# Row loads of the last third in 128 equal runs, and four weight columns copied two steps later, in a Fourier-transform and gated-product kernel

## The chip, the cores and the metric

The kernel runs on one core of one Trainium2 chip. The metric is device time in microseconds (us) of one execution. Where several executions are quoted, the number is their median. The profile of a kernel is one execution of it, and its span is some 1.7 to 2.8 us shorter than the device time of that execution.

## The reference, cut to what matters

```python
# x: (8, 3008, 256) f32; w_in: (256, 2048) f32; w_out: (2048, 256) f32
X = np.fft.fft(np.fft.fft(x, axis=1), axis=2).real.astype(np.float32)
t = X.reshape(8 * 3008, 256)
h = t @ w_in
g = h * np.cos(h)
return (g @ w_out).astype(np.float32)
```

## The kernel before

Both Fourier transforms are done as matmuls in f32. The transform over the 256 channels is folded into w_in ahead of time: TensorE multiplies w_in by cosines and sines, which gives Wc and Ws ("fold_sin", "fold_cos"). The transform over the 3008 rows is a set of matmuls against constant matrices MC. VectorE first folds each row with its mirror rows, so that a quarter of the rows, 752, is left to transform. After that come 376 steps, most of them 4.75 us long. A step makes two blocks of h, the cosine, the product and the second matmul.

Row s of a quarter lies on partition p in slot m. The first 512 rows lie four to a partition. The last third (rows 512 to 767, of which those after 752 are zeroed in MC) lies in two halves of 64 partitions. The function that says so, the mask that goes with it, and the load:

```python
def _row_of(m):
    p = np.arange(128)
    return 4 * p + m if m < 4 else 512 + 4 * (p % 64) + 2 * (p // 64) + m - 4

    low = np.arange(128) < 64          # in _dft_consts: the rows with v = row % 4 < 2
# ... cut ...
    def load_x(b, gather=True):
        # ... cut: tiles; GpSimd gathers the two mirrored sides (indirect loads) ...
        for j, row in ((0, 0), (3, HALF)):
            pin(eng.dma_start(out=L[j][:, 0 : 4 * ND], in_=xrows(b, row, 4, 128, 4)))
            pin(eng.dma_start(
                    out=L[j][:, 4 * ND :],
                    in_=bass.AP(tensor=xt, offset=x.offset + (b * SEQ + row + 512) * ND,
                        ap=[[2 * ND, 2], [4 * ND, 64], [1, 2 * ND]])))
```

The outer dimension of that last pattern has size 2: two sets of 64 runs of 2 rows (2 KB). The loads are issued on SyncE's queue (SP) in this order: half of w_in, the four row loads of batch 0, the other half of w_in, two of the constant matrices, w_out, the other two.

Channel 128 has no partition left in the 128-row array. Its weights are the last row of Ws. Small DMAs issued by GpSimd (POOL) turn that row into columns, "wex". They stand inside fold_sin, so POOL meets them in program order:

```python
    def fold_sin(q, tag="H"):
        ps = fold_mms(q, 128, tag)
        act(Ws[:, q * 512 : (q + 1) * 512], ps)
        for f in range(4):
            c = q * 512 + f * 128
            pin(nc.gpsimd.dma_start(out=wex[q][:, f : f + 1], in_=Ws[127:128, c : c + 128]))
```

POOL also makes weight sums ("WT") and, in every step, four sums of G that TensorE waits for. The rows of channel 128 come by a chain of loads on SP. It loads one channel element by element, writes it to DRAM and reads it back in the layout of the rows ("xs"). The first read is cut in two because of the two halves above:

```python
        def copy(j, s0, s1, row, step):        # in load_ext: x1 <- x, 8 partitions each
            spin(out=rows[j][:, s0:s1], in_=bass.AP(tensor=xt,
                    offset=x.offset + row * ND + 128,
                    ap=[[SEQ * ND, NB], [step * ND, s1 - s0], [1, 1]]))
        # ... cut: five such copies, four of them of 768 elements for each of 8 batches ...
            for j in range(4):                  # in turn_ext
                spin(out=xe_dr[j], in_=rows[j][:, 0:768])
            for j in range(4):
                spin(out=xs[:, j, :, 0:4], in_=xe_dr[j][:, 0:512].rearrange("b (p m) -> p b m", m=4))
                pairs = xe_dr[j][:, 512:768].rearrange("b (q h m) -> h q b m", h=2, m=2)
                for h in range(2):
                    spin(out=xs[64 * h : 64 * h + 64, j, :, 4:6], in_=pairs[h])
```

This chain feeds one fold on POOL ("xs<-xs") and one transform on TensorE ("MC,xe") in step 12. Wherever I write "the channel-128 chain", I mean these loads on SP.

Of the kernel before, what the change touches and what calls it, by code (L numbers as in the profile page):

```python
# [18 lines left out]
SEQ = 3008  # L19
ND = 256  # L20
# [16 lines left out]
def _row_of(m):  # L37

    p = np.arange(128)
    return 4 * p + m if m < 4 else 512 + 4 * (p % 64) + 2 * (p // 64) + m - 4  # L40


def _dft_consts():

    low = np.arange(128) < 64
    every = low | True
    out = np.zeros((128, 4, MW), np.float64)
    for kodd in range(2):
        for ri in range(2):
            fn = np.cos if ri == 0 else np.sin  # L50
            c = 0
            for m, keep, n in (
                (0, every, NH),
                (4, low, NH),
                (2, every, NH),
                (4, ~low, NH),
                (1, every, NE),
                (3, every, NE),
                (5, every, NE),
            ):  # L60
                s = _row_of(m)
                k = 2 * np.arange(n) + kodd
                v = fn(2.0 * np.pi * ((s[:, None] * k[None, :]) % SEQ) / SEQ)
                v[s > RUN] = 0.0
                v[s == 0] *= 0.5
                v[s == RUN] *= 0.5 if ri == kodd else 0.0
                v[~keep] = 0.0
                out[:, 2 * kodd + ri, c : c + n] = v
                c += n
    return out.reshape(128, -1).astype(np.float32)  # L70
# [22 lines left out]
def _row_consts():  # L93

    neg = SEQ - _row_of(3)
    last = neg.copy()
    last[0] = SEQ - 4
    return np.stack(
        [neg, SEQ - _row_of(5), HALF - _row_of(3), HALF - _row_of(5), last], axis=1
    ).astype(np.uint32)  # L100
# [3 lines left out]
def kernel(  # L104
# [11 lines left out]
    n_tiles = (n_cols + TW - 1) // TW  # L116

    MC_dr = nc.inline_tensor(_dft_consts(), name="dft_mats")
    CC_dr = nc.inline_tensor(_chan_consts(), name="chan_mats")
    PK_dr = nc.inline_tensor(_pick_consts(), name="pick_mats")  # L120
# [14 lines left out]
    xt = x.tensor  # L135

    def xrows(b, row, step, n, rows=6):

        return bass.AP(
            tensor=xt,  # L140
            offset=x.offset + (b * SEQ + row) * ND,
            ap=[[step * ND, n], [1, rows * ND]],
        )
# [6 lines left out]
    def gather_x(b, L, j, short):  # L150

        if short:
            c, part = 2 * j - 1, slice(0, 2 * ND)
        else:
            c = 4 if j == 1 and b == NB - 1 else 2 * j - 2
            part = slice(2 * ND, 6 * ND)
        pin(
            nc.gpsimd.indirect_dma_start(
                out=L[j][:, part],
                out_offset=None,  # L160
                in_=xflat,
                in_offset=bass.IndirectOffsetOnAxis(ap=ix[:, c : c + 1], axis=0),
                element_offset=b * SEQ * ND,
            )
        )

    def spin(**kw):
        pin(nc.sync.dma_start(**kw))  # L168
# [3 lines left out]
    def load_x(b, gather=True):  # L172
        L = [
            spool.tile([128, 6 * ND], FP, tag=f"xl{j}", bufs=1, name=f"xl{j}")
            for j in range(4)
        ]
        if gather:
            for j, short in GATHERS:
                gather_x(b, L, j, short)
        eng = nc.gpsimd if b == 1 else nc.sync  # L180
        for j, row in ((0, 0), (3, HALF)):
            pin(eng.dma_start(out=L[j][:, 0 : 4 * ND], in_=xrows(b, row, 4, 128, 4)))
            pin(
                eng.dma_start(
                    out=L[j][:, 4 * ND :],
                    in_=bass.AP(
                        tensor=xt,
                        offset=x.offset + (b * SEQ + row + 512) * ND,
                        ap=[[2 * ND, 2], [4 * ND, 64], [1, 2 * ND]],
                    ),  # L190
                )
            )
        return L
# [23 lines left out]

    load_w1(0)
    L_first = load_x(0)
    load_w1(1)  # L220

    def w1_cols(h, c0, c1):
        half = c0 // 1024
        return w1[h, half][:, c0 - half * 1024 : c1 - half * 1024]
# [3 lines left out]
    for kodd in range(2):  # L228
        for ri in range(2):
            m = cpool.tile([128, MW], FP, tag=f"MC{ri}{kodd}", name=f"MC{ri}{kodd}")  # L230
# [3 lines left out]
        if kodd == 0:  # L234
            spin(
                out=w2.rearrange("p (q c) -> p q c", c=ND),
                in_=moe_w_out.rearrange("(q p) c -> p q c", p=128),
# [22 lines left out]
    xe_dr = dpool.tile([4, NB, 768], FP, tag="xe", name="xe_dr")  # L260
    r4_dr = dpool.tile([1, NB], FP, tag="r4", name="r4")

    def bank(tag):
        bufs = 3 if tag == "H" else 1
        return ppool.tile([128, 512], FP, tag=tag, bufs=bufs, name=tag)
# [3 lines left out]
    def mm(out_, lhsT, rhs, start, stop=True):  # L269
        pin(  # L270
            nc.tensor.matmul(  # L271
                out_, lhsT=lhsT, rhs=rhs, start=start, stop=stop, skip_group_check=True
            )
        )
# [7 lines left out]
    def act(o, i, func=AF.Copy, **kw):  # L282
        pin(nc.scalar.activation(out=o, in_=i, func=func, **kw))  # L283


    def fold_mms(q, part, tag):

        ps = bank(tag)
        for h in range(2):
            mm(  # L290
                ps,
                CC[:, h * 256 + part : h * 256 + part + 128],
                w1_cols(h, q * 512, (q + 1) * 512),
                h == 0,
                h == 1,
            )
        return ps

    def fold_sin(q, tag="H"):
        ps = fold_mms(q, 128, tag)  # L300
        act(Ws[:, q * 512 : (q + 1) * 512], ps)
        for f in range(4):
            c = q * 512 + f * 128
            pin(nc.gpsimd.dma_start(out=wex[q][:, f : f + 1], in_=Ws[127:128, c : c + 128]))

    def fold_cos(q, tag="H"):
        ps = fold_mms(q, 0, tag)
        act(Wc[:, q * 512 : (q + 1) * 512], ps)
# [254 lines left out]
    def turn_ext():  # L563
        rows, xs = state["rows"], state["xs"]
        with nc.allow_non_contiguous_dma(reason="runs of rows"):
# [3 lines that stand above are left out]
                spin(  # L569
                    out=xs[:, j, :, 0:4],  # L570
                    in_=xe_dr[j][:, 0:512].rearrange("b (p m) -> p b m", m=4),
                )
                pairs = xe_dr[j][:, 512:768].rearrange("b (q h m) -> h q b m", h=2, m=2)
                for h in range(2):
                    spin(out=xs[64 * h : 64 * h + 64, j, :, 4:6], in_=pairs[h])

    def fold_ext():
        xs = state["xs"]
# [380 lines left out]
    def warm(n):  # L959

        w = bank("M")
        for _ in range(n):
            mm(w, zero[:, 0:128], zero[:, 0:1].to_broadcast([1, 512]), True)

    for q in range(2):
        fold_sin(q)
        fold_cos(q)
    warm(3)
    EO, ops = fold_x(L_first, nc.vector, 1)

    def fold_now(keys):
        for key in keys.split():
            ops[key, 0]()
# [3 lines left out]

    fold_now("z1 z3 c0 e0 o0 c3 e3 c2 e2 E2 x1 c1 e1 E0 EO0")
    fold_sin(2)
    fold_cos(2)  # L980
    R_even.first("pA")
    R_even.second("pB")
    xb = fold_first(L_first)
# [17 lines left out]
    def at(t, fn):  # L1001
        events.append((t, len(events), fn))

    T = PERIOD
# [67 lines left out]
    for t, fn in (  # L1072
        (-1.8, I_even.side),
        (-0.1, I_even.unfold),
        (0.0, I_even.plus),
        (0.95, lambda: fold_sin(3, "pD")),
        (1.0, lambda: fold_now("EO1")),
        (1.1, I_even.minus),
        (3.0, lambda: state.update(wc3=fold_mms(3, 0, "pA"))),
        (4.81, lambda: act(Wc[:, 1536:2048], state.pop("wc3"))),  # L1080
        (0.2, R_even.minus),
        (0.3, x_even.minus),
        (4.7, lambda: fold_now("EO3")),
        (3.1, lambda: R_odd.first("pB")),
        (3.2, lambda: R_odd.second("pC")),
        (T + 0.95, R_odd.side),
        (T + 0.96, R_odd.unfold),
        (T + 1.0, R_odd.plus),
        (T + 1.1, R_odd.minus),
        (T + 3.1, lambda: I_odd.first("pD")),  # L1090
        (T + 3.2, lambda: I_odd.second("pC")),
        (2 * T + 0.1, I_odd.side),
        (2 * T + 0.15, I_odd.unfold),
        (2 * T + 0.2, I_odd.plus),
        (2 * T + 0.3, I_odd.minus),
    ):
        at(t, fn)
    at(-1.5 * T, load_ext)
    at(-T, turn_ext)
    e0 = 12 * T  # L1100
    at(e0 + 1.35, fold_ext)
# [103 lines left out]
```

## Time and profile before

| before | us |
|---|---|
| three runs: 1972.84 to 1975.46, median | 1972.84 |
| span of the profiled execution | 1971.3 |
| TensorE (PE) busy | 1940.8 |

The profile's page gives the busy time of each engine, and rows of 40 slices of 49 us with the busy share in tenths. PEclk is the granted clock of TensorE in tenths of full speed.

```profile
span 1971.3 us, 28169 instructions
...
PE 1940.8 (98%) x8858; PEld 1654.1 (84%) x8858; DVE 1418.2 (72%) x2354; ACT 1452.6 (74%) x2791; POOL 1355.8 (69%) x1869
...
PEclk8999999999999999999999999999999999999999
```

TensorE is busy nearly always. Of its 30.5 us of idle time, 18.5 us lie in the first 122 us. The timeline of the kernel before, read one engine at a time and put in order of time, shows what happens there (a selection of its lines). Each line has start, duration, engine, source line, operation, output<-inputs and count; the brackets give the engine's idle time just before and what ended it. SPq is the issuing of DMAs on SyncE's queue.

```profile
7.25 10.76 SPq L168 DMA_DIRECT2D w<-in_moe_w_in_dram  x2
...
19.46 0.17 DVE L354 COPY e<-xl 128x6 f32<-128x6 f32 x1 [18.56 <-DMA xl<-in_x_dram]
27.69 0.17 DVE L354 COPY e<-xl 128x6 f32<-128x6 f32 x1 [6.34 <-DMA xl<-in_x_dram]
28.71 6.01 PE L271 MATMUL H<-w,CC 128*128 128x512 f32 x8 [10.93 <-DMA w<-in_moe_w_in_dram]
34.55 1.45 PE L271 MATMUL pA<-MC,e 128*128 128x189 f32 x8
35.39 55.76 SPq L168 DMA_DIRECT2D x<-in_x_dram  x5
44.13 1.03 PE L271 MATMUL H<-Rr,Wc 128*128 128x256 f32 x4
...
55.80 0.56 POOL L304 DMA_DIRECT2D wex<-Ws  x1 [5.38 <-ACT vs L283]
65.28 1.22 PE L271 MATMUL pB<-G,WT 128*128 128x256 f32 x2 [4.03 <-POOL G L280]
...
91.27 13.82 SPq L168 DMA_DIRECT2D xe_dr<-x  x4
105.14 8.42 SPq L168 DMA_DIRECT2D xs<-xe_dr  x12
117.58 0.39 POOL L280 TENSOR_TENSOR xs<-xs 128x96 f32<-128x96 f32 x1
118.98 2.09 PE L271 MATMUL H<-MC,xe 128*8 128x189 f32 x28
```

Rows of batch 0 are complete at 19.46 us on one side and at 27.69 us on the other. TensorE waits 10.93 us for the second half of w_in. The first row transform starts at 34.55 us and step 0 at 44.13 us. In step 0, TensorE waits another 4.03 us for POOL: the line at 65.28 us is its first matmul with a sum of G. POOL is late because it stood at the last four wex copies. The bracket of the copy at 55.80 us names ScalarE; a gather of batch 1 had landed just before (55.24 against 55.38 us), and the copy waits for the semaphore of that gather too, because it counts on the same one. The other three copies start 0.3 us after the last increment of another gather each (56.45, 57.97 and 58.61 us). The last lines are the channel-128 chain: its last load is issued at 113.56 us and landed at 115.11 us, in time for the fold at 117.58 us.

The view of windows gives, for chosen stretches, the busy time of each engine, the granted clock, the DMA engines' busy share and their rate.

```profile
core 0: us, PE busy (x) PEld busy (x) DVE busy (x) ACT busy (x) POOL busy (x), PEclk, DMA share, GB/s
16.00:18.00 2.00, 1.78 (x6) 0.39 (x4) 0.00 (x0) 0.60 (x1) 1.76 (x4) 1.00 0.16 54
...
17.80:28.70 10.90, 0.00 (x0) 0.03 (x1) 2.90 (x6) 0.00 (x0) 0.70 (x4) 0.59 0.95 289
61.30:65.30 4.00, 0.02 (x1) 0.03 (x1) 3.22 (x6) 2.26 (x4) 3.76 (x7) 0.86 0.35 86
65.30:71.00 5.70, 5.70 (x14) 4.53 (x15) 1.98 (x3) 1.09 (x2) 5.46 (x10) 0.50 0.26 24
```

Two gaps of TensorE are seen, of 10.9 and 4.0 us. Behind each the clock is at one half for some time, so the gap costs more than its length. In the trace the half-clock stretches are 19.77 to 33.42 us and 64.14 to 70.97 us; 4.7 and 5.7 us of them lie behind the gaps.

### The profile page before, as it was taken

Reading aid. Unit: us, or ns where it says so; the run is one execution under the profiler, and the core shown is the slowest. Engines: PE = TensorE matmul, PEld = TensorE weight load, DVE = VectorE, ACT = ScalarE, POOL = GpSimd, SP = SyncE. Lnnn points to the kernel's source line nnn. Section 1 sums busy time; section 2 is a strip of 40 time slices with the busy share of each in tenths; the row PEclk is TensorE's granted clock in tenths of the full one; section 3 lists DMA queues with packets and bytes.
Section 4 is the critical chain, followed back from the end, with each engine's and each line's share of the span. In section 5 each row is a group of like instructions: output and inputs, shape, how many; then the busy total and the mean of one; then the engine's idle time right before and its main releaser. Section 6 shows DMA issues by size and latency. Waiting matters only on the chain.

```text
span 1971.3 us, 28169 instructions
## 1 busy us (share of the span) xinstructions
PE 1940.8 (98%) x8858; PEld 1654.1 (84%) x8858; DVE 1418.2 (72%) x2354; ACT 1452.6 (74%) x2791; POOL 1355.8 (69%) x1869
## 2 busy tenths in 40 slices
PE   7999999999999999999999999999999999999998
PEld 3788888888888888888888888888888888887887
DVE  4577767777677766777677776777777776777777
ACT  1677777777777777777777777777777777777775
POOL 3777758776677766777667776777767776555654
PEclk8999999999999999999999999999999999999999
DMA  9721210002100021000210103001030110000101
GB/s 243 58 24 21 61 43 19 15 14 56 44 19 11 16 70 32 18 16 12 79 29 12 22 7 88 11 20 27 7 83 11 25 19 15 14 11 13 21 12 22
DMA packets 260925, 66.16 MB, mean 34 GB/s; under 512 B 248047, under 2 KB 250871, under 8 KB 260776
## 3 DMA queue, kind: packets, MB, share of 16 engines
q1 hardware_dynamic: 253160, 49.93, 13.8%
q0 software_dynamic: 5440, 14.17, 2.4%
q8 instruction: 70, 1.15, 0.2%
q14 instruction: 79, 0.65, 0.1%
q10 hardware_dynamic: 2176, 0.26, 0.1%
HBM read 39.48 MB, written 24.79 MB: 33 GB/s over the span
## 4 chain that ended last, share of the span: by engine, by line
PE 91%; DVE 3%; DMA 2%; ACT 1%; SPq 1%; issue 1%; POOL 1%; DVEq 0%; POOLq 0%
PE H L271 36%; PE pC L271 16%; PE pB L271 16%; PE pD L271 16%; PE pA L271 8%; DMA w<-in_moe_w_out_dram 1%; DVE G L724 1%; ACT G L283 1%; SPq L168 1%; DMA xl<-in_x_dram,ix 1%; DVE v L277 0%; DVE G L277 0%; POOL G L280 0%; DVE M L277 0%; ACT E L283 0%
## 5 line engine op out<-in xcount | busy, mean ns | idle before, releaser
L280 POOL TENSOR_TENSOR G<-G 128x256 f32<-128x256 f32 x1500 | 1076.9, 728 | 561.4 <-DVE G L724 470.8
L724 DVE SCALAR_TENSOR_TENSOR G<-H,G 128x512 f32<-128x512 f32 x376 | 256.7, 683 | 268.9 <-ACT G L283 268.9
L277 DVE TENSOR_TENSOR G<-H,G 128x512 f32<-128x512 f32 x376 | 260.0, 691 | 220.5 <-ACT G L283 217.5
L283 ACT ACTIVATE G<-H 128x512 int32<-128x512 f32 x376 | 224.5, 597 | 237.0 <-DVE G L277 235.6
L271 PE MATMUL pC<-G,WT 128*128 128x256 f32 x1504 | 388.2, 380 | 2.0 <-DVE u L277 1.9
L271 PE MATMUL H<-Ir,Ws 127*128 127x256 f32 x1504 | 388.5, 380 | 0.7 <-ACT E L283 0.7
L271 PE MATMUL H<-Rr,Wc 128*128 128x256 f32 x1504 | 387.0, 380 | 0.8 <-ACT H L283 0.7
L283 ACT ACTIVATE H<-Rb,wex 128x256 f32<-128x256 f32 x752 | 360.0, 479 | 25.9 <-DVE G L724 10.7
L283 ACT ACTIVATE E<-H 128x512 f32<-128x512 f32 x376 | 224.1, 596 | 203.6 <-PE H L271 200.8
L271 PEld LDWEIGHTS H<-Rr,Wc 128*128 128x128 f32 x1504 | 283.7, 190 | 48.6 <-ACT H L283 2.7
L271 PEld LDWEIGHTS pC<-G,WT 128*128 128x128 f32 x1504 | 284.4, 190 | 46.1 <-PE H L271 5.8
L271 PEld LDWEIGHTS H<-Ir,Ws 127*128 127x128 f32 x1504 | 282.9, 190 | 45.4 <-ACT E L283 6.4
L283 ACT ACTIVATE G<-G,halfpi 128x512 f32<-128x512 f32 x376 | 269.5, 717 | 1.5 <-DVE G L277 1.5
L277 DVE TENSOR_TENSOR G<-E,H 128x512 f32<-128x512 f32 x376 | 254.9, 678 | 5.4 <-PE H L271 3.6
L277 DVE TENSOR_TENSOR M<-G,M 128x512 f32<-128x512 f32 x376 | 257.6, 685 | 0.0
L724 DVE SCALAR_TENSOR_TENSOR G<-G,M 128x512 f32<-128x512 f32 x376 | 254.0, 676 | 0.5 <-ACT M L283 0.3
L283 ACT ACTIVATE M<-M,halfpi 128x512 f32<-128x512 f32 x376 | 246.2, 655 | 0.4 <-DVE M L277 0.3
L271 PE MATMUL pB<-G,WT 128*128 128x256 f32 x752 | 227.7, 384 | 4.8 <-POOL G L280 4.7
L283 ACT ACTIVATE M<-G 128x512 int32<-128x512 f32 x376 | 224.4, 597 | 0.0
L271 PE MATMUL pD<-G,WT 128*128 128x256 f32 x752 | 224.2, 380 | 0.0
L271 PE MATMUL pD<-G,w 128*128 128x256 f32 x752 | 223.9, 379 | 0.0
L271 PE MATMUL pB<-G,w 128*128 128x256 f32 x752 | 223.7, 379 | 0.1
(134 smaller groups left out, 1798.3 us busy)
## 6 DMA issues: line engine op xcount, KB each, us to landing
out_dram<-ot SPq DMA_DIRECT2D x496, 32.0 KB
xl<-in_x_dram SPq DMA_DIRECT2D x14, 512.0 KB
out_dram<-ot SPq DMA_DIRECT2D x256, 2.0 KB
MC<-dft_mats SPq DMA_DIRECT2D x4, 943.5 KB
Rb<-r SPq DMA_DIRECT2D x10, 376.0 KB
xl<-in_x_dram SPq DMA_DIRECT2D x14, 256.0 KB
w<-in_moe_w_in_dram SPq DMA_DIRECT2D x4, 512.0 KB
w<-in_moe_w_out_dram SPq DMA_DIRECT2D x1, 2048.0 KB
```

Source lines behind the costliest of these rows:

```text
L168: pin(nc.sync.dma_start(**kw))
L271: nc.tensor.matmul(out_, lhsT=lhsT, rhs=rhs, start=start, stop=stop, skip_group_check=True)
L277: pin(nc.vector.tensor_tensor(out=o, in0=a, in1=b, op=op))
L280: pin(nc.gpsimd.tensor_tensor(out=o, in0=a, in1=b, op=op))
L283: pin(nc.scalar.activation(out=o, in_=i, func=func, **kw))
L724: nc.vector.scalar_tensor_tensor(out=o, in0=h, scalar=TWO_PI, in1=c, op0=ALU.mult, op1=ALU.mult)
```

## The change

The first part puts the last third of the rows in pairs of one partition each, so that every row load has 128 equal runs. Only the constants change with it: the mask, and the row table of the gathers, which is built from the same function. The second part takes the last wex copies out of the fold, so that POOL does not stand at them before the first sums of G. The copies of q = 3 come two steps later, those of the others after the cosine fold of the same q.

```diff
 def _row_of(m):
-    return 4 * p + m if m < 4 else 512 + 4 * (p % 64) + 2 * (p // 64) + m - 4
+    return 4 * p + m if m < 4 else 512 + 2 * p + m - 4
-    low = np.arange(128) < 64
+    low = np.arange(128) % 2 == 0
 ...  # load_x
-                    out=L[j][:, 4 * ND :],
-                    in_=bass.AP(tensor=xt, offset=x.offset + (b * SEQ + row + 512) * ND,
-                        ap=[[2 * ND, 2], [4 * ND, 64], [1, 2 * ND]]),
+                    out=L[j][:, 4 * ND :], in_=xrows(b, row + 512, 2, 128, 2)
 ...  # fold_sin: the loop over f moves into a function of its own
+    def turn_last(q):
         for f in range(4):
 ...  # turn_ext
-                pairs = xe_dr[j][:, 512:768].rearrange("b (q h m) -> h q b m", h=2, m=2)
-                for h in range(2):
-                    spin(out=xs[64 * h : 64 * h + 64, j, :, 4:6], in_=pairs[h])
+                spin(out=xs[:, j, :, 4:6],
+                    in_=xe_dr[j][:, 512:768].rearrange("b (p m) -> p b m", m=2))
 ...  # order of the program
+        turn_last(q)                              # q = 0, 1, after fold_cos(q)
+    turn_last(2)                                  # after fold_cos(2)
         (0.95, lambda: fold_sin(3, "pD")),
+        (2 * T + 0.35, lambda: turn_last(3)),
```

More of the change, by code (lines that the diff above doesn't have):

```diff
@@ L184, in load_x @@
                 eng.dma_start(
-                    out=L[j][:, 4 * ND :],
-                    in_=bass.AP(
-                        tensor=xt,
-                        offset=x.offset + (b * SEQ + row + 512) * ND,
-                        ap=[[2 * ND, 2], [4 * ND, 64], [1, 2 * ND]],
-                    ),
+                    out=L[j][:, 4 * ND :], in_=xrows(b, row + 512, 2, 128, 2)
                 )
@@ L572, in turn_ext @@
                 )
-                pairs = xe_dr[j][:, 512:768].rearrange("b (q h m) -> h q b m", h=2, m=2)
-                for h in range(2):
-                    spin(out=xs[64 * h : 64 * h + 64, j, :, 4:6], in_=pairs[h])
+                spin(
+                    out=xs[:, j, :, 4:6],
+                    in_=xe_dr[j][:, 512:768].rearrange("b (p m) -> p b m", m=2),
+                )
     def fold_ext():
```

## The prediction

> **What bounds it.** From 71 us on the kernel is TensorE-bound: PE is busy 1940.8 of 1971.3 us (page, part 1); in windows of 50 us from 160 us on it loses at most 0.5 us each (1.1 once). No PE work is removed, so only the start can give time. Windows of 2 us and the waits show what is lost there: 17.8 to 28.7 us idle for the second half of w_in (10.9 us, released by that DMA), 61.3 to 65.3 us idle for a POOL sum (4.0 us), and granted clock 0.5 behind both (19.8 to 33.4 and 64.1 to 71.0 us).
>
> **What the change does.**
> 1. *Row loads.* Each 256 KB load of the last third has a DRAM side of 2 x 64 runs. The trace's semaphore records show two data increments for each of batch 0's two (18.2, 19.4; 26.4, 27.6 us) where full loads show 16. Transfers queued behind show 14 early increments and two late: w_in's third piece 15.4 to 16.9 against 27.6 and 28.6 us, w_out 33.2 to 33.9 against 39.5 and 40.4. So two engines carry each load and hold up all behind it. The Trainium skill, "DMA: Bandwidth & Descriptors", section "Why a DMA increments its semaphore by 16 and not by 1", says that the slowest dimension of both sides sets the number of engines: 2 before, 16 after; the trace agrees for before. Two engines lose about 224 KB of extra work each, about 11 us by estimate at the 21 KB/us they made up to 28.6 us.
> 2. *Channel-128 columns.* The last four wex copies stand before POOL's weight sums; POOL waits there from 50.4 to 59.45 us (5.4, 0.4, 1.0 us in the timeline) for gathers of batch 1. They move behind step 0's sums; POOL does eight weight sums (3.6 us) first and is there when VectorE delivers.
> 3. Four fewer small xs loads on SP, off the path.
>
> **Estimate.** First row tiles complete at 12 us (now 19.5), the other side at 15 (27.7), w_in at 19 (28.7), w_out at 30 (40.4). The first transform (PE, 34.55 us) starts at 23 to 25, limited by PE's fold of w_in (3.5 us at full clock, 6 at half): gain 9 to 11.5 us. The chain to step 0 is engine work and shifts whole. Then the 4.0 us wait and 3 us lost to the half clock nearly go, 1 us staying for ACT: gain 5 to 6.5. Together 15 to 18 us. Later row loads are made 8 steps ahead: no gain.
>
> **Predicted: 1956.5 us (-0.8%), 1951 to 1964 in 8 of 10. Over 2% faster 1%, within 98%, slower 1%.**
>
> **What would show it.** Small row loads with 16 increments close together; w_in by 20 us; DVE's first fold at 11 to 14 us; first transform at 22 to 26; no POOL wait for wex near 50 us; PE's wait for POOL under 1 us; clock 1.0 from 25 us; the rhythm of 4.75 us reached at 53 to 56 us instead of 71.
>
> **What would make it wrong.** The clock falling in a shorter PE gap ("TensorE: Matmul & The Clock Gate", Part 1: a window of about 3.4 us; here it fell 2 us into the first gap and 2.9 into the second), costing 2 to 3 us; gathers of batch 0 slowed by w_in; element-wise channel-128 loads (55.8 us of issue on SP) shifting less than PE, so that step 12's fold waits.

## The result, and the profile after

| | before | after |
|---|---|---|
| median of four runs each, same rounds | 1973.85 | 1957.01 |
| lowest and highest of the changed kernel's runs | | 1956.48, 1960.7 |
| span of the profiled execution | 1971.3 | 1954.1 |

The ratio is 0.9918, with an interval of 0.9901 to 0.9935. Every ratio in this document is the mean time of one kernel's fast runs over that of the other kernel's fast runs of the same rounds, so it is not quite the ratio of the medians that are quoted. The result is correct. The gain is 0.8%, within 2%, and the predicted 1956.5 us is 0.5 us off. The profile that was kept of the changed kernel is of an execution other than these four, whose spans were 1954.4 to 1958.9 us.

The page of the kernel after, with the same three rows:

```profile
span 1954.1 us, 28165 instructions
...
PE 1936.6 (99%) x8858; PEld 1650.5 (84%) x8858; DVE 1418.9 (73%) x2354; ACT 1453.6 (74%) x2791; POOL 1357.7 (69%) x1869
...
PEclk9999999999999999999999999999999999999999
```

TensorE's busy time falls by 4.2 us though its instructions are as many as before. That fits the stretches at half clock, which are gone: the fold of w_in's second half, for one, takes 3.80 instead of 6.01 us. The other 13.0 of the 17.2 us of span are idle time that is gone.

The timeline of the kernel after, one engine at a time, in order of time (a selection of its lines):

```profile
5.01 1.15 SPq L168 DMA_DIRECT2D w<-in_moe_w_in_dram  x2
11.87 0.17 DVE L352 COPY e<-xl 128x6 f32<-128x6 f32 x1 [10.96 <-DMA xl<-in_x_dram]
15.57 0.17 DVE L352 COPY e<-xl 128x6 f32<-128x6 f32 x1 [1.81 <-DMA xl<-in_x_dram]
17.25 3.80 PE L266 MATMUL H<-w,CC 128*128 128x512 f32 x8
21.82 1.55 PE L266 MATMUL pA<-MC,e 128*128 128x189 f32 x8 [0.77 <-DVE e L331]
24.09 52.95 SPq L168 DMA_DIRECT2D x<-in_x_dram  x5
31.57 1.02 PE L266 MATMUL H<-Rr,Wc 128*128 128x256 f32 x4
...
48.56 2.15 POOL L302 DMA_DIRECT2D wex<-Ws  x4
48.81 0.59 PE L266 MATMUL pB<-G,WT 128*128 128x256 f32 x2
54.80 0.70 PE L266 MATMUL pB<-G,WT 128*128 128x256 f32 x2 [0.19 <-POOL G L275]
77.16 13.87 SPq L168 DMA_DIRECT2D xe_dr<-x  x4
91.08 6.32 SPq L168 DMA_DIRECT2D xs<-xe_dr  x8
99.91 0.39 POOL L275 TENSOR_TENSOR xs<-xs 128x96 f32<-128x96 f32 x1
101.32 2.09 PE L266 MATMUL H<-MC,xe 128*8 128x189 f32 x28
```

The fold of w_in's second half has no wait at all now, and the first transform waits 0.77 us for VectorE. The first matmul with a sum of G, the one that waited 4.03 us, is at 48.81 us and waits for nothing; the one of the next step waits 0.19 us. Subtracting the starts of the same lines tells where the span went:

| point on TensorE | before | after | earlier by |
|---|---|---|---|
| first row transform (pA) | 34.55 | 21.82 | 12.73 |
| step 0 (H<-Rr,Wc) | 44.13 | 31.57 | 12.56 |
| transform of channel 128 (MC,xe) | 118.98 | 101.32 | 17.66 |
| end of the span | 1971.3 | 1954.1 | 17.2 |

So 12.6 us come from before step 0, 5.1 us between step 0 and step 12, and nothing after. The windows of the kernel after:

```profile
core 0: us, PE busy (x) PEld busy (x) DVE busy (x) ACT busy (x) POOL busy (x), PEclk, DMA share, GB/s
17.80:21.80 4.00, 3.25 (x8) 1.06 (x6) 3.90 (x8) 1.20 (x2) 1.79 (x6) 1.00 1.03 395
47.90:56.00 8.10, 7.52 (x33) 5.66 (x33) 6.73 (x13) 5.95 (x12) 7.83 (x14) 1.00 0.89 3
```

Both stretches that stood at half clock have full clock now. In the first, VectorE with its folds is the busiest engine (3.90 of 4.00 us).

The trace's semaphore records fit. Each of batch 0's two small row loads counted up by 2 before (18.2 and 19.4 us; 26.4 and 27.6 us) and counts up by 16 now, close together (11.0 to 11.8 us; 15.2 to 15.5 us). The last piece of w_in is complete at 18.2 us instead of 29.8, and w_out at 29.4 instead of 40.4.

### The profile page after: what moved, and what is told of

Read it like the earlier page. It is cut to its first block, busy times and chain, and to the rows that moved or that the text cites. A ratio compares the mean times of both kernels' runs of the same rounds, so it can differ in the third digit from the quotient of the medians.

```text
span 1954.1 us, 28165 instructions
## 1 busy us (share of the span) xinstructions
PE 1936.6 (99%) x8858; PEld 1650.5 (84%) x8858; DVE 1418.9 (73%) x2354; ACT 1453.6 (74%) x2791; POOL 1357.7 (69%) x1869
## 3 DMA queue, kind: packets, MB, share of 16 engines
q8 instruction: 70, 1.15, 0.2%
## 4 chain that ended last, share of the span: by engine, by line
PE 92%; DVE 3%; ACT 1%; issue 1%; POOL 1%; DVEq 0%; POOLq 0%
PE H L266 37%; PE pB L266 16%; PE pC L266 16%; PE pD L266 16%; PE pA L266 8%; DVE G L723 1%; ACT G L278 1%; POOL G L275 1%; DVE v L272 0%; DVE G L272 0%; DVE M L272 0%; ACT E L278 0%; DVE ab L272 0%; DVE u L272 0%; DVE ot L831 0%
## 5 line engine op out<-in xcount | busy, mean ns | idle before, releaser
L278 ACT ACTIVATE H<-Rb,wex 128x256 f32<-128x256 f32 x752 | 360.2, 479 | 25.9 <-DVE G L723 10.7
L266 PE MATMUL pA<-G,w 128*128 128x256 f32 x752 | 223.8, 379 | 0.0
```

The source lines that it names most:

```text
L266: nc.tensor.matmul(out_, lhsT=lhsT, rhs=rhs, start=start, stop=stop, skip_group_check=True)
L278: pin(nc.scalar.activation(out=o, in_=i, func=func, **kw))
```

## The experiments

The kernel before was run in every round beside the others. Its medians in the three groups of runs were 1974.48 (11 runs), 1974.33 (9) and 1973.32 (11). Six of the kernels below compute a wrong result, because their loads bring other values than the constants expect; they are used for their times alone.

My first theory, from the prediction, had two independent causes: the number of DMA engines that carry a small row load (worth 9 to 11.5 us), and the place of the wex copies (worth 5 to 6.5 us). Rivals: the rows' part gives everything; what matters is that runs lie adjoining in DRAM, not how many engines carry them; it is the stalled issuing queue that delays the rest.

### e1: the rows alone

The changed kernel with the wex copies back in their old place. The result is correct.

```diff
@@ fold_sin
+        for f in range(4):
+            c = q * 512 + f * 128
+            pin(nc.gpsimd.dma_start(out=wex[q][:, f : f + 1], in_=Ws[127:128, c : c + 128]))
@@ all calls of turn_last removed
```

> The changed kernel with the last wex copies put back before POOL's weight sums; only the row loads are new. My theory (two separate gains, the rows worth 11 to 13 us, the move of wex worth the rest): POOL waits for the gathers of batch 1 again, but these land at 40.5 to 44.2 us in the changed kernel (55.2 to 58.6 before), so the wait costs only 2 to 4 us: 1959 to 1963 us, 10 to 14 us faster than before, PE waiting 2.5 to 4 us for POOL at pB. Rival (the moved wex copies carry the gain, the rows matter little): 1967 us or more.

Measured: median 1958.96 us (1956.6 to 1959.69), ratio to before 0.9911 (0.9893 to 0.9929). The rows alone give about all of the gain. The timeline of e1 on POOL and TensorE shows why so little is missing:

```profile
43.04 0.54 POOL L299 DMA_DIRECT2D wex<-Ws  x1 [3.50 <-DMA xl<-in_x_dram,ix]
...
52.70 0.70 PE L266 MATMUL pB<-G,WT 128*128 128x256 f32 x2 [2.93 <-POOL G L275]
```

The wait in step 0 is still there, but 2.93 us instead of 4.03 us. One half-clock stretch of 3.41 us follows it, where the kernel before had 6.83 us. In this profile the transform of channel 128 starts at 105.30 us, 4.0 us after the changed kernel's. 0.8 us of that was there at step 0 already (32.37 against 31.57 us), so the old place of wex costs 3.2 us in this one execution. Against the kernel before, the stretch from step 0 to step 12 is 1.9 us shorter in e1 (13.7 us earlier at step 12, 11.8 us at step 0), so the rows give a part of that gain as well. The medians are only 1 to 2 us apart, and the ratios overlap.

### e2: the wex copies alone

The kernel before with only the wex copies moved. The result is correct.

```diff
@@ fold_sin of the kernel before: the loop over f moved to turn_last
+        turn_last(q)                     # after fold_cos(q), q = 0, 1, 2
+        (2 * T + 0.35, lambda: turn_last(3)),
```

> The kernel before with only the wex copies moved. My theory: the start up to step 0 stays as it was (first transform at 34.5 us, w_in complete near 29 us), the wait of 4.0 us at pB and the half clock behind it go: 1965 to 1968 us, 5 to 7 us faster than before. Rival (the wait at pB was covered by another wait that ends as late, so that nothing is won): within 2 us of before.

Measured: median 1974.41 us (1970.74 to 1977.16), ratio 0.9993 (0.9974 to 1.0013). I had expected several us of gain; there is none. So the two parts of the gain don't add as the prediction had it. The timeline of e2 on TensorE and POOL shows that the gain was made and given back:

```profile
60.17 0.59 PE L271 MATMUL pB<-G,WT 128*128 128x256 f32 x2
66.16 0.70 PE L271 MATMUL pB<-G,WT 128*128 128x256 f32 x2 [0.18 <-POOL G L280]
...
115.92 0.39 POOL L280 TENSOR_TENSOR xs<-xs 128x96 f32<-128x96 f32 x1 [4.60 <-DMA out_dram<-ot]
116.72 3.77 PE L271 MATMUL H<-MC,xe 128*8 128x189 f32 x28 [3.96 <-POOL xe L280]
```

POOL is in time in the first steps: TensorE's first matmul with a sum of G (60.17 us) doesn't wait, and the next waits 0.18 us. Then in step 12 POOL waits 4.60 us, TensorE 3.96 us, and the transform takes 3.77 instead of 2.09 us, since the clock falls for 3.41 us from 116.54 us on. The wait is labelled with the stores of "ot". They are issued just behind the last xs load on the same queue, and the fold reads nothing but xs, so I read the label as the last xs load. The semaphore records fit: its last increment came at 115.53 us, 0.4 us before the fold started. SP issued that load up to 113.93 us, as in the kernel before (113.56 us). Without the wait of step 0, POOL came to the fold at 111.32 us (115.92 less 4.60) instead of 117.58, and the data were not there. That is a reading of the trace; e6 tests it.

### e3 and e4: 16 and 4 engines with interleaved runs

The changed kernel, with the pattern of the small row loads replaced. Both give wrong results.

```diff
-                    out=L[j][:, 4 * ND :], in_=xrows(b, row + 512, 2, 128, 2)
+                    ... ap=[[2 * ND, 16], [32 * ND, 8], [1, 2 * ND]]     # e3
+                    ... ap=[[2 * ND, 4], [8 * ND, 32], [1, 2 * ND]]      # e4
```

> The changed kernel with the small row loads strided again, but with 16 x 8 runs on the DRAM side instead of 2 x 64 (the rows come in another order, so the result is wrong on purpose; the times do not depend on values). My theory (the size of the outer dimension sets the number of engines): 16 increments per load, as fast as the changed kernel: 1955 to 1960 us. Rival (the gain comes from the 256 KB now being one contiguous stretch of DRAM, or from one dimension less): the loads are slow again and the time goes back to 1964 us or more.

> As the run with 16 x 8 runs, with 4 x 32 runs (wrong result on purpose). My theory: four engines carry each load, each has 96 KB more than an even share from the two loads of batch 0; at 21 to 26 KB per us that holds back everything behind by 4 to 5 us: 4 increments per small load, w_in complete at about 22 us, first transform at 25 to 27 us, 1959 to 1963 us. Rival (any strided form is as slow as 2 x 64): 1966 us or more; rival (only two engines are a special bad case): 1957 us.

Measured: e3 1957.91 us (1957.17 to 1960.54), ratio 0.9911 (0.9893 to 0.9929). e4 1968.92 us (1964.7 to 1973.99), ratio 0.9961 (0.994 to 0.9982), a miss of my 1959 to 1963. In e3 the runs that follow one another stand 32 KB apart in DRAM, and it is as fast as the changed kernel: contiguity does not matter here. e4 showed 4 semaphore increments for each small load and its last w_in piece at 27.2 us. I had expected a delay that falls as the excess bytes of an engine fall, and it falls more slowly. That is one half of the miss. The other is the wait that e2 showed: in e4's profile TensorE waits 6.88 us for the channel-128 chain in step 12, with a half-clock stretch of 6.83 us. The profiles of e5, e11, e12 and e8 below have such waits too (1.29, 3.71, 4.66 and 7.37 us), so the times of these kernels hold two delays, and only the arrivals tell about the first. Against the kernel before, e4 changes the number of engines and the order of the runs at once, so a series with adjoining runs was made as well.

### e5, e11 and e12: 2, 4 and 8 engines with adjoining runs

The changed kernel, with the 128 runs cut into 2, 4 or 8 blocks of adjoining runs. A row is skipped between blocks, so that the pattern can't be written with one dimension. All give wrong results.

```diff
-                    out=L[j][:, 4 * ND :], in_=xrows(b, row + 512, 2, 128, 2)
+                    ... ap=[[129 * ND, 2], [2 * ND, 64], [1, 2 * ND]]    # e5
+                    ... ap=[[65 * ND, 4], [2 * ND, 32], [1, 2 * ND]]     # e11
+                    ... ap=[[33 * ND, 8], [2 * ND, 16], [1, 2 * ND]]     # e12
```

> The changed kernel in everything (wex moved, four xs loads fewer), but each small row load reads two blocks of 64 adjoining runs with one row left out between them, so that its DRAM side has an outer dimension of 2 and yet is contiguous within 128 KB (rows shifted by one in the second block: wrong result on purpose). Theory (the size of the outer dimension sets the number of engines): two increments per small load, w_in complete at 27 to 30 us as before, first transform at 32 to 35 us; about as slow as the run with 4 x 32 runs or the kernel before: 1968 to 1974 us. Rival (contiguity of the DRAM side is what counts): w_in by 20 us and 1957 to 1960 us.

> As the run with two blocks, with four blocks of 32 adjoining runs (wrong result on purpose). The run with 4 x 32 interleaved runs had w_in complete at 27 us, where my estimate from bytes was 22 us. If the interleaving was to blame: w_in by 21 to 23 us here. If four engines as such cost that much: 25 to 27 us again.

> As the run with two blocks, with eight blocks of 16 adjoining runs (wrong result on purpose): 8 increments for each small load, 32 KB more than an even share on eight engines; by bytes w_in at 19 to 20.5 us; if a smaller count of engines costs more than its bytes, as with four, 22 us or more.

Measured: e5 1969.77 us (1967.82 to 1975.23), ratio 0.9981 (0.9959 to 1.0002). e11 and e12 were one look each, of unknown state: 1970.07 and 1967.51 us. What the looks are for is the arrival times in the trace, with the changed kernel as the last row. "Excess" is worked out: two loads of 256 KB over k engines, less the even share over 16.

| engines (increments seen) | excess per engine | last piece of w_in | later than with 16 | first transform |
|---|---|---|---|---|
| e5: 2 | 224 KB | 29.3 us | 11.1 us | 34.67 us |
| e11: 4 | 96 KB | 25.8 us | 7.6 us | 30.24 us |
| e12: 8 | 32 KB | 22.9 us | 4.7 us | 27.37 us |
| changed kernel: 16 | 0 | 18.2 us | 0 | 21.82 us |

With four engines, interleaved runs (e4, 27.2 us) are no faster than adjoining ones (25.8 us). With two engines, adjoining runs are as slow as the interleaved runs of the kernel before (29.3 and 29.8 us). With more engines the delay falls, so it is the number of engines that does it. It does not fall in proportion to the excess. By the prediction's rate of 21 KB/us for each engine, the three excesses would be 10.7, 4.6 and 1.5 us. The first agrees and the other two are 3 us short. Part of it is that the other engines are late too: in e12 the first 8 increments of the last piece came at 18.8 to 20.2 us, where all 16 of the changed kernel came at 17.9 to 18.2. Individual packets of 2 KB lasted 84 to 86 ns in the mean in the changed kernel and 142 to 163 ns in some stretches of e11 and e12. Why they do is open.

### e6: the wex copies alone, with a short channel-128 chain

The kernel e2, with the channel-128 loads reading adjoining elements (other values, so wrong). This makes the chain short and leaves the rest as it is.

```diff
-                    ap=[[SEQ * ND, NB], [step * ND, s1 - s0], [1, 1]],
+                    ap=[[SEQ * ND, NB], [1, s1 - s0]],
```

> The kernel before with the wex copies moved, and with the four element-wise loads of channel 128 replaced by contiguous loads of other values (wrong result on purpose): the channel-128 chain on SP then ends long before step 12. Theory (what the move of wex wins near 61 us is given back at step 12, where PE waits 4.0 us for xs and loses the clock for 3.4 us): no wait at the fold of xs, no half clock near 117 us, 1965 to 1969 us, 5 to 9 us faster than before. Rival (the move of wex wins nothing even without that wait): within 2 us of before.

Measured: median 1967.81 us (1967.28 to 1968.09), ratio 0.9965 (0.9951 to 0.9978), against 0.9993 of e2. The timeline of e6:

```profile
35.30 5.33 SPq L168 DMA_DIRECT2D x<-in_x_dram  x5
...
113.12 2.09 PE L271 MATMUL H<-MC,xe 128*8 128x189 f32 x28
```

The loads from x take 5.33 us of issue instead of 57.17 in e2, and the transform in step 12 waits for nothing. So the move of the wex copies is worth some 5 to 7 us in the old kernel, if the channel-128 chain is out of the way: 6 to 7 us by the times, and by the profiles 5.2 us between step 0 and step 12 (118.98 less 113.12, less 0.67 us already there at step 0). It is the chain that took the gain of e2 back. The short chain without the move of wex was not run; in the kernel before the fold does not wait for the chain, so no gain is expected of it, but that is not shown.

### e7: the xs loads cut in two again

The changed kernel with 12 xs loads instead of 8. The result is correct.

```diff
-                spin(out=xs[:, j, :, 4:6],
-                    in_=xe_dr[j][:, 512:768].rearrange("b (p m) -> p b m", m=2))
+                for h in range(2):
+                    spin(out=xs[64 * h : 64 * h + 64, j, :, 4:6],
+                        in_=xe_dr[j][:, 512 + 128 * h : 640 + 128 * h].rearrange("b (p m) -> p b m", m=2))
```

> The changed kernel with each of the four merged xs loads cut in two again (8 xs loads of 64 partitions for the last third, as before; the result is right). In the changed kernel the last xs load is issued by 97.4 us and the fold of xs comes at 99.9 us without a wait, so the four loads saved (about 2.1 us of issue on SP) are near the limit. Theory: xs ends about 2 us later, POOL waits 0.5 to 2.5 us at the fold of xs, 1957 to 1961 us. Rival (the merge has slack to spare): no wait, same time as the changed kernel within 0.5 us.

Measured: median 1956.29 us, ratio 0.9912 (0.9895 to 0.993). The five runs are of two kinds: 1955.63, 1955.94 and 1956.29, and 1961.92 and 1961.96. The profile fell on one of the second kind. The timeline of e7:

```profile
105.92 3.79 PE L266 MATMUL H<-MC,xe 128*8 128x189 f32 x28 [4.27 <-POOL xe L275]
```

In that execution TensorE waits 4.27 us for the chain in step 12, as in e2, and 3.41 us of half clock follow. But the other three runs are as fast as the changed kernel. The changed kernel itself has such a second kind: of its ten runs in two groups, six lie between 1955.7 and 1957.4 us and four between 1959.3 and 1964.3 us. So what cutting the xs loads costs by itself is not settled. What is settled is that the chain is close to the path. In the changed kernel's profile its last load is issued at 97.40 us, the last increment comes at 99.19 us and the fold starts at 99.91 us. Where the fold waited (e2, e7), it started 0.4 us after the last increment, so only some 0.3 us are to spare. And the chain itself varies from one execution to the next: with 8 xs loads and all 16 engines for the rows, the last increment came at 95.56 us in e3, 98.33 in e10 (below), 99.19 in the changed kernel and 102.40 in e1.

### e8: the small row loads on another queue

The kernel before, with batch 0's two small loads issued from ScalarE's queue. The result is correct.

```diff
-                eng.dma_start(
+                (nc.scalar if b == 0 else eng).dma_start(
```

> The kernel before with the two small row loads of batch 0 issued from the ACT queue instead of SP; still 2 x 64 runs. Theory (the two engines' own work is what everything waits for, whoever issues it): still two increments each, w_in complete at 25 to 29 us and w_out at 37 to 41 us; within 5 us of before (1968 to 1976 us). Rival (the loads block SP's queue, and it is the queue behind them that suffers): w_in by 21 us, w_out by 32 us, 1957 to 1964 us.

Measured: median 1972.93 us (1967.5 to 1977.4), ratio 0.9981 (0.9958 to 1.0005). The last piece of w_in is complete at 27.9 us (29.8 in the kernel before) and w_out at 38.8 us (40.4), both in the range of the theory. The timeline of e8 shows that this is not the clean test that was meant:

```profile
2.68 1.47 SPq L182 DMA_DIRECT2D xl<-in_x_dram  x2
19.44 0.80 SPq L168 DMA_DIRECT2D w<-in_moe_w_in_dram  x2
```

SP issued the second half of w_in only at 19.44 us, because its first piece counts on the semaphore of the first small load, which landed at 19.43 us. So these arrivals don't tell the queue from the engines. The first half of w_in does. SP issued it at 1.63 and 2.21 us, with nothing ahead of it on its own queue but the row table and one 256 KB load. Its two pieces show 14 increments at 6.1 to 7.2 and at 7.8 to 8.8 us, and two at 10.4 and 10.7 and at 13.6 and 14.0 us; in the kernel before all had come by 6.6 and 8.6 us. The Trainium skill, "DMA: Bandwidth & Descriptors", section "Issuing engines are not separate DMA queues", says that DMAs of all issuers run on the same 16 engines. This run agrees: the small loads of ScalarE's queue hold up two sixteenths of what SP's queue issues. That SP's queue stalls as well in the kernel before (10.76 us for two pieces of w_in) is a second effect. It is not what the completion waited for there: 14 increments of the last piece had come by 21.8 us, and the two others came at 28.9 and 29.8 us.

### e9 and e10: the channel-128 loads on 16 partitions, beside the changed kernel

If the chain is that close to the path, a shorter chain should make the changed kernel's runs alike. A sequence and its second half lie HALF rows apart, so two of the four loads fit into one pattern with an outer dimension of 16. The Trainium skill, "DMA: Bandwidth & Descriptors", section "Rules for kernel authors", says that an outermost dimension of size c under 16 confines a DMA to at most c engines; it was 8 here, and the traces agree: each of the four large loads counted up by 8 in the changed kernel, each of the two in e9 by 16. e9 is the changed kernel with that, and correct. e10 is the changed kernel, unchanged, in the same rounds.

```diff
-            copy(0, 0, 768, 0, 1)
-            copy(1, 1, 768, SEQ - 1, -1)
-            copy(2, 0, 768, HALF, -1)
-            copy(3, 0, 768, HALF, 1)
+            copy(fwd, 0, 768, 0, [[HALF * ND, 2 * NB]], 1)
+            copy(back, 1, 768, HALF - 1, [[HALF * ND, 2 * NB]], -1)
@@ cut: fwd and back are 16 partitions each of x1, xe_dr is [2, 16, 768], two copies of one element,
@@ and xs is read from the matching half of xe_dr
```

> The changed kernel with the same rule applied to the loads of channel 128: the four element-wise loads of 8 partitions become two of 16 (rows 0 and 1504 of each batch are one stride apart), so each should run on 16 engines instead of 8; the result is right. Theory (the channel-128 chain is the next wall, and in some runs of the changed kernel PE waits for it and loses the clock): SP issues the last xs load at 60 to 85 us instead of 97 us, no wait at the fold of xs in any run, 1955 to 1957.5 us, and none of the runs near 1960 us that the changed kernel has one in four of. Rival (the chain is never on the path of the changed kernel): same times with the same spread as the changed kernel in this job.

> The changed kernel once more, for a comparison on the same chip: 1956 to 1958 us in most runs; where a run is 2 us or more slower, the channel-128 chain came late (theory); in a run with a profile near 1960 us POOL waits at the fold of xs, in one near 1957 us it does not.

Measured: e9 median 1954.55 us (1954.3 to 1955.12, four runs), ratio to before 0.9904 (0.989 to 0.9918). e10 median 1957.94 us (1955.74 to 1964.31, six runs), ratio 0.9931 (0.9916 to 0.9946). The timeline of e9:

```profile
24.14 28.85 SPq L168 DMA_DIRECT2D x<-in_x_dram  x4
57.56 9.52 SPq L168 DMA_DIRECT2D xe_dr<-x  x2
67.17 5.61 SPq L168 DMA_DIRECT2D xs<-xe_dr  x8
99.80 0.39 POOL L275 TENSOR_TENSOR xs<-xs 128x96 f32<-128x96 f32 x1
```

The last xs load is issued at 72.78 us, 27 us before the fold, instead of 97.40. The four runs lie within 0.8 us, where the changed kernel's lie within 8.6 us. The mean of e9 (1954.63 us) is 0.24% below that of e10 (1959.31 us). e9 is the fastest of the kernels run here: each of its four runs is below every run of the kernel before and of the changed kernel. The profiles of e9 and e10 are of undisturbed executions and agree to 0.1 us in step 12 (101.21 and 101.32 us); their spans are 1952.5 and 1954.0 us. Of these last 1.5 us, 0.1 us is there at step 12, 0.5 us by step 76, and 0.7 us lies behind TensorE's last matmul, so the wait for the chain has no part in them. What e9 gains in the mean is that none of its four runs is of the slower kind.

## Why the prediction was right or wrong

The time was right: 1956.5 us against 1957.01 us. That it is only 0.5 us off is in part luck: one of the two terms came out above its range, the other at the lower end of its own, and ten runs of the changed kernel spread over 8.6 us. Most of the steps were right too, but not what the second part of the gain was put down to.

**The rows: right, and a little larger.** Predicted were arrivals at 12, 15, 19 and 30 us for the first side, the other side, w_in and w_out. Measured were 11.87, 15.57, 18.2 and 29.4. The first transform was to start at 23 to 25 us and started at 21.82, so the term of 9 to 11.5 us measured 12.7 us. The step that was off is "limited by PE's fold of w_in": TensorE had done that fold by 21.05 us, and VectorE's folds released the transform, with 0.77 us of wait. The clock did not fall in the shorter gap.

The Trainium skill, "DMA: Bandwidth & Descriptors", section "Why a DMA increments its semaphore by 16 and not by 1", says that the largest number up to 16 that divides the slowest dimension of both sides is the number of engines that carry a load. The traces agree: outer dimensions of 2, 4, 8, 16 and 128 gave 2, 4, 8, 16 and 16 increments. e3 and e5 show that the number of engines, and not the adjoining of runs, decides; e8 shows that loads issued from another queue are held up as well.

**The sizing by excess bytes: right for 2 engines by luck.** The prediction said that two engines carry 224 KB too much, at 21 KB/us 11 us. The delay was 11.6 us. The same sum fails for 4 and 8 engines (7.6 and 4.7 us measured, 4.6 and 1.5 from the sum), so it is not the law behind it. What adds some 3 us there is open.

**Step 0's wait and the clock behind it: right in size.** 5 to 6.5 us were predicted after step 0, 5.1 us were measured (17.66 less 12.56). POOL's wait for wex near 50 us is gone, TensorE's wait for POOL is 0.00 us in step 0 and 0.19 us in the next, and the clock stays up. The Trainium skill, "TensorE: Matmul & The Clock Gate", Part 1, gives a free-running window of 3413 ns for the clock. The half-clock stretches of all runs agree, but for the last one of each profile, which the end of the record cuts: 3.41, 6.83, 10.24 and 13.65 us, one to four windows. In the kernel before they begin inside the gap, 2.0 and 2.9 us after TensorE stopped; in e1 and e7 they begin 0.8 and 0.7 us behind it. So such a gap is paid in its own length and then at half speed up to the end of a window: 4.7 of 13.65 us and 5.7 of 6.83 us in the kernel before. The gaps of 0.77 us in the changed kernel and of 1.29 us in e5 brought no half clock.

**What the second term was put down to: wrong.** The prediction wrote "Then the 4.0 us wait and 3 us lost to the half clock nearly go", as the gain of moving the wex copies, and added it to that of the rows. e2 shows that the move alone gains nothing, because the channel-128 chain on SP then holds up step 12; e6 shows that it gains some 5 to 7 us when the chain is short. e1 shows that the rows alone gain all but some 1 to 3 us: of the 5.1 us between step 0 and step 12, its profile has 1.9 us without any move of wex, because the gathers for which POOL stands at wex land 12.6 us earlier or more (42.5 to 46.0 us) and step 0 comes only 11.8 us earlier: the wait shrinks to 2.93 us, with one window of half clock. So the term of 5 to 6.5 us held some 2 us of the rows. The two parts share one limit. The row loads move that limit too: in the changed kernel SP's queue is not stalled (issuing two pieces of w_in took 1.15 us instead of 10.76), so the channel-128 loads start at 24.09 instead of 35.39 us. The rows' part is what makes room for the wex part. How much the wex part is worth on top of the rows, the runs do not settle; the profiles of e1 and the changed kernel say 3.2 us, the medians 1 to 2.

**"Four fewer small xs loads on SP, off the path": wrong.** They end a chain that has some 0.3 us to spare in the changed kernel (e7). The prediction named this chain among what could make it wrong, "shifting less than PE, so that step 12's fold waits". That is what happened in e2 and in the profiled execution of e7. TensorE came 17.7 us earlier to step 12 and the chain only 16.2 us (113.56 to 97.40), so the room from the last issue to the fold shrank from 4.0 to 2.5 us, of which the landing takes 1.8 us. That the slower four of the changed kernel's ten runs are this wait is argued, not shown: no profile of such a run was taken. It is supported by e9, whose chain is ready 27 us ahead and whose runs are all alike, and by the granted clock: 0.997, 0.997, 0.998 and 0.999 in the four slower runs against 0.999 to 1.0 in the six others, and 0.998 in the run of e7 whose profile shows the wait.

## What to carry to other kernels

Look at the outer dimension of every load in the critical start of a kernel, on both sides: one that divides into few engines delays not only itself but all that is queued behind it, and the number of semaphore increments shows it at a glance. When two changes each remove a wait, test each alone, since the next wait may take one gain back; e2 looked worthless by time, and its profile showed the gain being made near 60 us and lost at 117 us. When a kernel's runs spread more than its neighbours', look for a chain with little room, and give it room: e9 won 0.24% in the mean that way without touching the busiest engine.

## What the Trainium skill lacked or had wrong

- "DMA: Bandwidth & Descriptors", section "Why a DMA increments its semaphore by 16 and not by 1", says how the number of engines follows from the pattern, but not what few engines cost the transfers queued behind. Here two 256 KB loads on 2, 4, 8 and 16 engines let the last piece of w_in, queued behind them, complete at 29.3, 25.8, 22.9 and 18.2 us, which is not in proportion to an engine's excess bytes.
- The same page does not say how long the issuing queue itself can be held up behind such loads. SP took 10.76 us to issue the next two pieces of w_in in the kernel before and 1.15 us in the changed one, and the loads of x behind them on that queue started 11.3 us later.
- The same page, section "Rules for kernel authors", says that an outer dimension under 16 confines a DMA to that many engines, and gives no time for loads element by element. Here the loads of one channel from x took 52.95 us of issue with an outer dimension of 8 (the changed kernel) and 28.85 us with 16 (e9), for the same elements in half as many large loads.
- None of the statements cited here was contradicted by a run.
